# Order of the first batch's loads, room for four pooled weight tiles, and ScalarE alone for the upper halves of the weights

## The chip, the cores and the metric

One core of one Trainium2 chip runs the whole program. The metric is the device time of one execution in microseconds (us), as the median of several runs. TensorE (PE) multiplies, ScalarE (ACT) and VectorE (DVE) do most of the element-wise work, GpSimd (POOL) takes a share of it, and SyncE (SP) issues nearly all transfers (DMA) from one in-order queue. Each engine runs its own instructions in the order in which the program lists them, and waits on semaphores for the others.

## The reference

Three blocks follow each other: an attention over `[4, 8, 576, 64]`, then two feed-forward blocks over its 2304 x 512 output.

```python
def _attn_ref(q, k, v):
    ...
    q_d = q.reshape(B, H, Sd, factor, D).mean(axis=3)      # factor = 4, the same for k and v
    out_d = sm_attn(q_d, k_d, v_d)
    out_up = np.repeat(out_d, factor, axis=2)
    ...
    mask = np.abs(pos[:, None] - pos[None, :]) < factor
    scores = scale * np.matmul(q, k.transpose(0, 1, 3, 2))
    scores = np.where(mask, scores, -1000000000.0)
    ...
    return (out_up + out_local).astype(np.float32)

def _moe_ref(x, w_in, w_out):
    h = x @ w_in                                           # 512 -> 2048
    g = np.where(h > 0.0, h, alpha * (np.exp(np.minimum(h, 0.0)) - 1.0))
    return (g @ w_out).astype(np.float32)

def _moe2_ref(x, w_gate, w_val, w_out):
    g = x @ w_gate                                         # 512 -> 1536
    silu = g * (1.0 / (1.0 + np.exp(-g)))
    val = x @ w_val
    return (silu * val @ w_out).astype(np.float32)
```

The five weight matrices arrive as float64; everything else is float32.

## The kernel before

**Attention.** A batch is cut into six units of 96 positions (`add_unit`). A unit loads queries and keys (L459), TensorE turns them (L495), a copy puts them into `qT`/`kT`, groups of four positions are summed into `sums` (L506 on VectorE, L508/L509 on GpSimd), banded scores follow (L523), a softmax over 32 columns (L535 to L558), a copy of the turned weights into a block-diagonal tile `bd`, and the product with the values (L577), copied to `xf` (tile `f`). The pooled attention has four head pairs per batch (`add_pooled`): values of four neighbours summed into `vs` (L596, L600/L601), scores (L617), maxima (L624), exponentials (L630), weights divided by their sums (L640, tile `pr`), turned (L655), times `vs` (L668), kept in `xdT`. `add_split` then adds the two (L688) into `x`, three units to a chunk of 288 positions.

**First feed-forward block.** There are eight chunks c, each with 16 steps f of 128 hidden columns. Chunk 0 (`add_whole`) is multiplied in full float32 (L735 into `h`, L740 into the accumulator), while the float64 weights are still arriving: two words per number are joined by ScalarE (L374, L377) and VectorE (L381, L383) into one float32 tile per matrix and step, 32 tiles in all ("a pair" below is one L381 and one L383). Chunks 1 to 7 use three fast products per matrix (L710 to L712) on weights split into an upper part (a rounded copy, `copy` at L276 on ScalarE or L278 on VectorE) and a remainder (L421 on GpSimd); `add_weight_split` makes both. `x` of these chunks is split in the same way (copy, L698), and so is `g` (copy, L790).

**Order.** Nothing is issued in the order of the loops. Each piece of work is a task with an engine (or a choice of two), an estimated cost and a due time. `Work.run` plays the tasks out once while the program is built: an engine that comes free takes the ready task with the smallest due time whose buffers have room, and that fixes each engine's instruction order. Due times of the first block count from `START` in steps (`time1`). `spans` gives, for batches 1 to 3, the steps between which their attention is due; `add_unit` holds their turns back until a named weight tile is joined (`then`). Once the first product of chunk 0 is placed, all attention work shares two PSUM banks, 4 and 5 (`att_bank`), which the joining of the weights uses too.

**Room.** 33 slots of 4 KB per partition (`w0` to `w32`) serve in turn as landing place for the first batch (`parts`, from slot `U0` on), for float64 words (14 slots), for joined tiles, and for split weights. The first batch's queries, keys, values and pooled values all have places of their own there, so its loads wait for no earlier work.

Of the kernel before, what the change touches and what calls it, by code (L numbers as in the profile page):

```python
# [228 lines left out]
def attention_moe_moe(ctx: ExitStack, tc: tile.TileContext, q, k, v, w_in, w_out, w_gate, w_val, w_o2, ident_in, mask_in, band_in, picks_in, out):  # L229
# [19 lines left out]
    NW = 2 * NF1 + 1  # L249
    U0, U1 = 6, 19  # L250

# [53 lines left out]

    START, STEP0, STEP, STEP2 = 62.0, 4.1, 3.7, 7.9
    order = [(c, f) for c in range(NC) for f in range(NF1)]
# [106 lines left out]

    def add_weight_split(key, due, w):

        wt[key] = w
        u = ww[key]
        add(COPIER, (0.6, 0.4), due - 2, lambda engine: copy(engine, w.t[:, 0], u.t.bitcast(F32)),
            reads=[u], writes=[w], second=0)  # L420
        return add("pool", 1.3, due - 1, lambda: nc.gpsimd.tensor_tensor(  # L421
            out=w.t[:, 1], in0=u.t.bitcast(F32), in1=w.t[:, 0], op=ALU.subtract), reads=[u, w], writes=[w])
# [15 lines left out]
            ("mx", [HALF, 2, 2], 4), ("nm", [HALF, 2, 2], 4), ("su", [HALF, 2, 2], 4),  # L438
            ("pr", [HALF, 2, 2, G], 2), ("prT", [HALF, 2, 2, G], 2),
            ("sm", [P, H, QB], 2), ("st", [P, H, 1], 2), ("pt", [P, H, QB], 1))}  # L440
# [23 lines left out]

    def add_unit(n, due, load_due, rows=None, after=(), then=(), late=0.0):

# [18 lines left out]

        add("sp", 2.0, load_due + 4.0, load_values, writes=[tv], nbytes=P * H * D * 4 * 1.9, after=after)
        if i == 0:
# [97 lines left out]

    def add_pooled(b, p, due, load_due, raws=None):

        if xdT[b] is None:
            xdT[b] = xdT_ring.new()
        vs = vs_ring.new()  # L590
        mx, nm, su, pr, prT = (small[n].new() for n in ("mx", "nm", "su", "pr", "prT"))
        qk = sums[b]
# [53 lines left out]
        add("dve", 0.6, due + 4, norm, reads=[su], writes=[su])  # L646
        add(EITHER, (0.78, 1.75), due + 4.3, weight, reads=[pr, su], writes=[pr])

# [31 lines left out]
    def add_split(n, xf, due):  # L680
        b, i = divmod(n, NU)
        c, j = divmod(n, UPC)
        if j == 0:
            xt[c] = x_ring.new()
        x, cols = xt[c], slice(j * U, (j + 1) * U)

        def both(engine, to):
            two(engine).tensor_tensor(  # L688
                out=to.rearrange("p a (g r) -> p a g r", r=R), in0=xf.t.rearrange("p (a g r) -> p a g r", a=NP, r=R),
                in1=xdT[b].t[:, :, i * GU:(i + 1) * GU].rearrange("p a (g o) -> p a g o", o=1).to_broadcast([P, NP, GU, R]),  # L690
                op=ALU.add)

        f = lambda: xf.t.rearrange("p (a t) -> p a t", a=NP)
        if c == 0:
            return add(EITHER, (0.8, 1.4), due, lambda engine: both(engine, x.t[:, :, 0, cols].bitcast(F32)), reads=[xf, xdT[b]], writes=[x])
        add(EITHER, (0.8, 1.4), due, lambda engine: both(engine, f()), reads=[xf, xdT[b]], writes=[xf])
        add(COPIER, (0.5, 0.6), due + 0.3, lambda engine: copy(engine, x.t[:, :, 0, cols], f()), reads=[xf], writes=[x], second=1)
        return add("pool", 1.1, due + 0.6, lambda: nc.gpsimd.tensor_tensor(  # L698
            out=x.t[:, :, 1, cols], in0=f(), in1=x.t[:, :, 0, cols], op=ALU.subtract), reads=[xf, x], writes=[x])
# [24 lines left out]
    def add_whole(f, due, acc, last):  # L724
# [18 lines left out]
        inner[:] = [add("pe", 4 * 0.51, due - STEP, gemm1, reads=[wi, x], writes=[h], after=inner)]  # L743
        add_weight_split(("in", f), time1(NF1 + f), w_slots.new(split_places))
        add("act", 0.45, due - URGENT, lambda: nc.scalar.activation(e.t, h.t[:, :T1], AF.Relu, scale=-1.0), reads=[h], writes=[e])
# [3 lines left out]
        last[0] = [add("pe", 4 * 0.51, due + STEP, gemm2, reads=[wo, g], writes=acc[0], after=last.get(0, ()), slack=1.0)]  # L749
        split_last = [add_weight_split(("out", f), time1(NF1 + f + 1), w_slots.new(split_places))]  # L750
        if f == NF1 - 1:
# [127 lines left out]
    with tc.manual_schedule():  # L879
# [10 lines left out]
        vals = [x for _ in range(NU // 2) for x in parts(2)]  # L890
        praws = [x for _ in range(NP) for x in parts(2)]
        for t in praws:
            t.t = t.t[:HALF].rearrange("p (h x) -> p h x", h=2)
# [21 lines left out]
        for n in range(NU):  # L915
            xfs[n] = add_unit(n, 4.0 * n, -40 + 2 * n, rows=(*rows[n], vals[n]), late=0.0 if n < UPC else 24.0)
            if n == 0:
                load_mask()
        for p in range(NP):
            add_pooled(0, p, 20.0 + 0.5 * p, -31 + p, raws=praws[2 * p:2 * p + 2])  # L920
        w1 = [(kind, f) for f in range(NF1) for kind in ("in", "out")]
# [10 lines left out]
        for n in range(UPC):  # L932
            made.append(add_split(n, xfs[n], 28.0 + 0.5 * n))
        spans = {1: (12, 24), 2: (41, 54), 3: (71, 84)}
        split = UPC
        for b in range(1, B):
            lo, hi = (time1(s) for s in spans[b])
            for i in range(NU):
                due = lo + (hi - lo) * i / NU
                xfs[b * NU + i] = add_unit(b * NU + i, due, due - 18, after=[words["in", 10 if b == 1 else NF1 - 1]],  # L940
                    then=[words["out", NF1 - 1]])
            for p in range(NP):
# [75 lines left out]
```

## Time and profile before

| what | us |
|---|---|
| median of 3 runs (1036.3 to 1039.7) | 1038.58 |
| the profiled execution, whole | 1041.44 |
| its span (first to last instruction in the trace) | 1039.6 |
| TensorE busy in the span | 998.2 |

The span is the part that the trace shows; the profiled execution took 1.8 us more than its span, and 2.9 us more than the median. TensorE is busy 96% of the span, and its granted clock averages 0.97 of full speed. A matmul at half clock counts as busy for twice as long, so what TensorE loses is seen in both: in idle time, and in stretches with a low clock.

### The profile page before, as it was taken

What the parts mean: (1) busy time and instruction counts of PE and PEld (TensorE: products, weight loads), DVE (VectorE), ACT (ScalarE), POOL (GpSimd) and SP (SyncE); (2) the same over time, 40 slices, a digit from 0 to 9 for tenths busy, and PEclk for the clock granted to TensorE, in tenths of its full rate; (3) what the DMA queues carried; (4) which work ended last, traced back from release to release, by engine and by line L of the source; (5) the groups of instructions that cost most, each with busy time, mean ns of one, the idle gap of its engine ahead of it and who ended that gap; (6) DMA issues with size and microseconds to landing.
All of it is one profiled execution on the core that took longest, in us unless ns stands there. A gap on an engine that the chain in (4) does not pass through costs nothing. (4 is left out here: it accounts for less than half of the span.)

```text
span 1039.6 us, 19385 instructions
## 1 busy us (share of the span) xinstructions
PE 998.2 (96%) x7540; PEld 870.3 (84%) x7540; DVE 526.0 (51%) x1080; ACT 404.1 (39%) x994; POOL 318.4 (31%) x375
## 2 busy tenths in 40 slices
PE   7679899989999999999999999999999999999998
PEld 5457689979999899899998888888888888888897
DVE  5978997786788777783124322232223222322232
ACT  4868455555555455555434521121112111211111
POOL 4432883572426343357258720010001000000000
PEclk8679999989999999999999999999999999999999
DMA  9995243464634564334024420020002000100000
GB/s 162 290 330 154 58 98 104 138 167 133 159 112 119 159 156 124 116 107 145 1 76 126 116 83 1 1 64 18 1 1 71 0 1 2 50 1 1 7 35 21
DMA packets 129004, 91.20 MB, mean 88 GB/s; under 512 B 73744, under 2 KB 116880, under 8 KB 128912
## 3 DMA queue, kind: packets, MB, share of 16 engines
q1 hardware_dynamic: 128768, 89.70, 31.6%
q8 instruction: 59, 0.97, 0.4%
q14 instruction: 33, 0.27, 0.1%
q10 hardware_dynamic: 144, 0.26, 0.1%
HBM read 71.06 MB, written 18.87 MB: 87 GB/s over the span
## 5 line engine op out<-in xcount | busy, mean ns | idle before, releaser
L710 PE MATMUL bank<-x,w 128*128 128x288 f32 (+2 forms) x928 | 318.1, 343 | 5.5 <-DVE e L783 5.4
L711 PE MATMUL bank<-x,w 128*128 128x288 f32 (+2 forms) x928 | 312.4, 337 | 0.4 <-POOL x L698 0.4
L712 PE MATMUL bank<-x,w 128*128 128x288 f32 (+2 forms) x928 | 311.6, 336 | 0.0
L856 DVE TENSOR_TENSOR e<-bank,e 128x512 f32<-128x512 f32 (+1 forms) x120 | 76.2, 637 | 260.7 <-ACT e L853 179.8
L710 PEld LDWEIGHTS bank<-x,w 128*128 128x128 f32 x928 | 175.8, 189 | 28.6 <-DVE e L783 8.5
L711 PEld LDWEIGHTS bank<-x,w 128*128 128x128 f32 x928 | 176.5, 190 | 17.2 <-POOL x L698 0.6
L712 PEld LDWEIGHTS bank<-x,w 128*128 128x128 f32 x928 | 176.3, 190 | 16.8
L790 POOL TENSOR_TENSOR g<-e,g 128x288 fp32r<-128x288 f32 x112 | 93.4, 834 | 175.2 <-ACT g L276 124.1
L710 PE MATMUL bank<-g,w 128*128 128x288 f32 x448 | 135.3, 302 | 0.0
L711 PE MATMUL bank<-g,w 128*128 128x288 f32 x448 | 132.8, 296 | 0.0
L712 PE MATMUL bank<-g,w 128*128 128x288 f32 x448 | 132.3, 295 | 0.0
L853 ACT ACTIVATE e<-bank 128x512 f32<-128x512 f32 (+1 forms) x60 | 33.2, 555 | 190.8 <-PE bank L712 190.8
L833 POOL TENSOR_TENSOR x<-x2r,x 128x512 fp32r<-128x512 f32 (+1 forms) x20 | 23.6, 1194 | 270.9 <-ACT x L832 270.9
L858 ACT CAST y<-e 128x512 fp32r<-128x512 f32 (+1 forms) x60 | 34.6, 577 | 154.3 <-DVE e L856 132.4
L710 PEld LDWEIGHTS bank<-g,w 128*128 128x128 f32 x448 | 84.8, 189 | 1.9 <-issue 1.2
L711 PE MATMUL bank<-w,y 128*128 128x512 f32 x216 | 85.7, 397 | 0.0
L711 PEld LDWEIGHTS bank<-g,w 128*128 128x128 f32 x448 | 85.3, 190 | 0.2
L710 PE MATMUL bank<-w,y 128*128 128x512 f32 x216 | 85.3, 395 | 0.0
L783 DVE SCALAR_TENSOR_TENSOR e<-e,bank 128x288 f32<-128x288 f32 x112 | 50.2, 449 | 69.4 <-ACT e L787 62.9
L712 PEld LDWEIGHTS bank<-g,w 128*128 128x128 f32 x448 | 85.0, 190 | 0.0
L712 PE MATMUL bank<-w,y 128*128 128x512 f32 x216 | 84.9, 393 | 0.0
L779 ACT ACTIVATE e<-bank 128x288 f32<-128x288 f32 x112 | 45.9, 410 | 100.1 <-PE bank L712 79.9
(115 smaller groups left out, 1410.3 us busy)
## 6 DMA issues: line engine op xcount, KB each, us to landing
wd<-mid SPq DMA_DIRECT2D x72, 128.0 KB
u<-wd SPq DMA_DIRECT2D x36, 256.0 KB
w<-in_moe_w_in_dram SPq DMA_DIRECT2D x16, 512.0 KB
w<-in_moe_w_out_dram SPq DMA_DIRECT2D x16, 512.0 KB
w<-in_moe_w_gate_dram SPq DMA_DIRECT2D x24, 256.0 KB
w<-in_moe_w_val_dram SPq DMA_DIRECT2D x24, 256.0 KB
w<-in_moe_w_out_dram SPq DMA_DIRECT2D x24, 256.0 KB
out_dram<-x2r SPq DMA_DIRECT2D x17, 256.0 KB
```

The costliest lines, as they stand in the source:

```text
L710: nc.tensor.matmul(ps, sh, mh, start=first, stop=False)
L711: nc.tensor.matmul(ps, sh, ml, start=False, stop=False)
L712: nc.tensor.matmul(ps, sl, mh, start=False, stop=last)
L779: nc.scalar.activation(e.t, h.t[:, :T1], AF.Relu, scale=-1.0)
L783: nc.vector.scalar_tensor_tensor(out=e.t, in0=e.t, scalar=-1.0, op0=ALU.add, in1=h.t[:, :T1], op1=ALU.max)
L790: add("pool", 0.82, due - URGENT, lambda e=e, g=g: nc.gpsimd.tensor_tensor(out=g.t[:, 1], in0=e.t, in1=g.t[:, 0], op=ALU.subtract), reads= ...
L833: add("pool", 1.3, due, lambda T=T, raw=raw, x=x: nc.gpsimd.tensor_tensor(out=x.t[:, 1, :T], in0=raw.t[:, :T], in1=x.t[:, 0, :T], op=ALU.s ...
L853: add("act", 0.6, due, lambda T=T, e=e, gate=gate: nc.scalar.activation(e.t[:, :T], gate.t[:, :T], AF.Sigmoid), reads=[gate], writes=[e], ...
L856: add("dve", 0.64, due, lambda T=T, e=e, x=x: nc.vector.tensor_tensor(out=e.t[:, :T], in0=x.t[:, :T], in1=e.t[:, :T], op=ALU.mult), reads= ...
L858: add("act", 0.6, due, lambda T=T, e=e, y=y: nc.scalar.copy(y.t[:, 0, :T], e.t[:, :T]), reads=[e], writes=[y])
```

## The change

The first batch's loads are asked for in another order: all queries and keys, then the rows for the pooled values, then the values of the units (`v_due`, and other due times in `add_pooled`). The four pooled weight tiles of the first batch get a place each in the slots (`probs`, so `U0` is 2 and `pr` has one buffer left for the later batches); their division by the sums, and the three additions into `x` of chunk 0, are VectorE's alone where VectorE or GpSimd could take them. The upper copies of the first block's weights are ScalarE's alone. `START` is 48 where it was 62, batch 1's attention is due in steps 10 to 20 where it was 12 to 24, and the turns of batches 1 to 3 are held back until the output tile of step 10 is joined, where it was that of step 15.

```diff
-    U0, U1 = 6, 19
+    U0, U1 = 2, 19
...
-    START, STEP0, STEP, STEP2 = 62.0, 4.1, 3.7, 7.9
+    START, STEP0, STEP, STEP2 = 48.0, 4.1, 3.7, 7.9
...
-    def add_weight_split(key, due, w):
+    def add_weight_split(key, due, w, copiers=COPIER):
...
-        add(COPIER, (0.6, 0.4), due - 2, lambda engine: copy(engine, w.t[:, 0], u.t.bitcast(F32)),
+        add(copiers, (0.62, 0.9)[:len(copiers)], due - 2, lambda engine="act": copy(engine, w.t[:, 0], u.t.bitcast(F32)),
...
-            ("pr", [HALF, 2, 2, G], 2), ("prT", [HALF, 2, 2, G], 2),
+            ("pr", [HALF, 2, 2, G], 1), ("prT", [HALF, 2, 2, G], 2),
...
-        add("sp", 2.0, load_due + 4.0, load_values, writes=[tv], nbytes=P * H * D * 4 * 1.9, after=after)
+        add("sp", 2.0, load_due + 4.0 if v_due is None else v_due, load_values, writes=[tv], nbytes=P * H * D * 4 * 1.9, after=after)
...
-        add(EITHER, (0.78, 1.75), due + 4.3, weight, reads=[pr, su], writes=[pr])
+        if b:
+            add(EITHER, (0.78, 1.75), due + 4.3, weight, reads=[pr, su], writes=[pr])
+        else:
+            add("dve", 0.78, due + 4.3, lambda: weight("dve"), reads=[pr, su], writes=[pr])
...
-            return add(EITHER, (0.8, 1.4), due, lambda engine: both(engine, x.t[:, :, 0, cols].bitcast(F32)), reads=[xf, xdT[b]], writes=[x])
+            return add("dve", 0.8, due, lambda: both("dve", x.t[:, :, 0, cols].bitcast(F32)), reads=[xf, xdT[b]], writes=[x])
...
-        add_weight_split(("in", f), time1(NF1 + f), w_slots.new(split_places))
+        add_weight_split(("in", f), time1(NF1 + f), w_slots.new(split_places), COPIER[:1])
...
+        probs = [x for _ in range(NP) for x in parts(1)]
...
-            xfs[n] = add_unit(n, 4.0 * n, -40 + 2 * n, rows=(*rows[n], vals[n]), late=0.0 if n < UPC else 24.0)
+            xfs[n] = add_unit(n, 4.0 * n, -40 + 2 * n, rows=(*rows[n], vals[n]), late=0.0 if n < UPC else 24.0,
+                v_due=-20.0 + n)
...
-            add_pooled(0, p, 20.0 + 0.5 * p, -31 + p, raws=praws[2 * p:2 * p + 2])
+            add_pooled(0, p, 16.0 + 0.5 * p, -28 + p, raws=praws[2 * p:2 * p + 2], pr=probs[p])
...
-        spans = {1: (12, 24), 2: (41, 54), 3: (71, 84)}
+        spans = {1: (10, 20), 2: (41, 54), 3: (71, 84)}
...
-                    then=[words["out", NF1 - 1]])
+                    then=[words["out", 10]])
```

(The same edit is made to the `out` weights.) What the planner makes of these numbers is seen in three places. First SyncE's queue, from its fourth load of the first batch on. `w_95` to `w_100` hold queries and keys of units 0 to 5, `w_101` to `w_103` values, `w_104` to `w_107` the rows for the pooled values. Before:

```order
L459 DMA w_96<-in_k_dram 112x8x64
L459 DMA w_101<-in_v_dram 16x8x64
L459 DMA w_101<-in_v_dram 13x8x64
L459 DMA w_101<-in_v_dram 32x8x64 x3
L459 DMA w_97<-in_q_dram 96x8x64
L459 DMA w_97<-in_k_dram 112x8x64
L459 DMA w_101<-in_v_dram 32x8x64 x4
L459 DMA w_98<-in_q_dram 96x8x64
L459 DMA w_98<-in_k_dram 112x8x64
L459 DMA w_102<-in_v_dram 32x8x64 x4
```

Now:

```order
L459 DMA w_97<-in_q_dram 96x8x64
L459 DMA w_97<-in_k_dram 112x8x64
L459 DMA w_98<-in_q_dram 96x8x64
L459 DMA w_98<-in_k_dram 112x8x64
L459 DMA w_99<-in_q_dram 96x8x64
L459 DMA w_99<-in_k_dram 112x8x64
L459 DMA w_100<-in_q_dram 96x8x64
L459 DMA w_100<-in_k_dram 112x8x64
L606 DMA w_104<-in_v_dram 72x2x256 x2
L606 DMA w_105<-in_v_dram 72x2x256 x2
L606 DMA w_106<-in_v_dram 72x2x256 x2
L606 DMA w_107<-in_v_dram 72x2x256 x2
```

All loads of values have moved behind these; the first weights still come after the last values, in both.

Second, VectorE just ahead of the additions into `x` of chunk 0 (L688 before, L692 now), on which the first product of the feed-forward block waits. Before, the first two CASTs being upper copies of weights:

```order
L278 CAST w_889<-w_763 128x512
L278 CAST w_894<-w_763 128x512
L381 SCALAR_TENSOR_TENSOR bank_887<-bank_887,w_799 128x512
L383 SCALAR_TENSOR_TENSOR w_799<-w_572,bank_887 128x512
L381 SCALAR_TENSOR_TENSOR bank_892<-bank_892,w_881 128x512
L383 SCALAR_TENSOR_TENSOR w_881<-w_579,bank_892 128x512
L278 COPY prT_920<-bank_919 72x288
L381 SCALAR_TENSOR_TENSOR bank_926<-bank_926,w_881 128x512
L383 SCALAR_TENSOR_TENSOR w_881<-w_587,bank_926 128x512
L381 SCALAR_TENSOR_TENSOR bank_944<-bank_944,w_917 128x512
L383 SCALAR_TENSOR_TENSOR w_917<-w_591,bank_944 128x512
L688 TENSOR_TENSOR x_969<-f_512,xdT_802 128x4x96
```

Now:

```order
L597 TENSOR_REDUCE vs_847<-w_107 72x128
L278 COPY prT_841<-bank_849 72x288
L558 STREAM_TRANSPOSE pt_867<-sm_539 128x256
L535 TENSOR_TENSOR sm_715<-bank_713,mask_86 128x128
L535 TENSOR_TENSOR sm_715<-bank_714,mask_86 128x128
L381 SCALAR_TENSOR_TENSOR bank_785<-bank_785,w_760 128x512
L383 SCALAR_TENSOR_TENSOR w_760<-w_518,bank_785 128x512
L540 TENSOR_REDUCE st_884<-sm_715 128x8
L692 TENSOR_TENSOR x_890<-f_579,xdT_807 128x4x96
L692 TENSOR_TENSOR x_890<-f_603,xdT_807 128x4x96
L692 TENSOR_TENSOR x_890<-f_682,xdT_807 128x4x96
```

Seven pairs stood ahead of the additions before, one does now; and the third addition, which stood in GpSimd's queue behind the additions for batch 1's pooled values, has moved here.

Third, TensorE where chunk 1 ends and chunk 2 begins (products with `g` belong to chunk 1, those with `x` to chunk 2; the rest is attention of later units). Before:

```order
L712 MATMUL bank<-g,w 128x288
L523 MATMUL bank<-kT,qT 32x32 x32
L577 MATMUL bank<-bd,vrows 64x96 x8
L495 MATMUL bank<-ident,rows 128x96 x4
L495 MATMUL bank<-ident,rows 128x112 x4
L523 MATMUL bank<-kT,qT 32x32 x32
L710 MATMUL bank<-x,w 128x288
L711 MATMUL bank<-x,w 128x288
```

Now:

```order
L716 MATMUL bank<-g,w 128x288
L577 MATMUL bank<-bd,vrows 64x96 x8
L523 MATMUL bank<-kT,qT 32x32 x32
L714 MATMUL bank<-x,w 128x288
L715 MATMUL bank<-x,w 128x288
```

The product with the values has moved ahead of the scores, and the second unit's turns and scores behind the first products of chunk 2.

## Rows read from the trace of the kernel before

**Rows 1.** The page, part 1: busy time of each engine.

```profile
PE 998.2 (96%) x7540; PEld 870.3 (84%) x7540; DVE 526.0 (51%) x1080; ACT 404.1 (39%) x994; POOL 318.4 (31%) x375
```

**Rows 2.** Windows: length; busy us of PE, PEld, DVE, ACT, POOL; PE clock; DMA.

```profile
9.49:56.20 46.71, 32.75 (x620) 26.02 (x620) 41.07 (x108) 34.01 (x99) 21.93 (x35) 0.66 1.01 257
106.30:134.86 28.56, 25.08 (x321) 18.81 (x320) 26.77 (x47) 11.89 (x28) 24.00 (x23) 0.94 0.29 64
580.00:1040.00 460.00, 455.48 (x2136) 376.66 (x2136) 123.81 (x197) 88.62 (x160) 32.16 (x28) 1.00 0.08 24
```

**Rows 3.** Timeline of TensorE, first feed-forward block: start us, duration us, instruction, idle before.

```profile
61.33 8.29 PE L735 MATMUL bank<-x,w 128*128 128x288 f32 x24 [4.90 <-POOL x L688]
69.45 2.10 PE L740 MATMUL bank<-g,w 128*128 128x288 f32 x8
71.39 2.10 PE L735 MATMUL bank<-x,w 128*128 128x288 f32 x8
```

**Rows 4.** Timeline of VectorE and GpSimd: additions into x, and what stands ahead.

```profile
55.18 1.02 DVE L688 TENSOR_TENSOR x<-f,xdT 128x384 f32<-128x384 f32 x2
...
58.00 0.72 POOL L600 TENSOR_TENSOR praw<-praw 72x256 f32<-72x256 f32 x1 [4.94 <-DMA praw<-in_v_dram]
...
60.42 0.86 POOL L688 TENSOR_TENSOR x<-f,xdT 128x384 f32<-128x384 f32 x1
```

**Rows 5.** Timeline of SyncE's queue: the first weight.

```profile
33.56 0.40 SPq L332 DMA_DIRECT2D w<-in_moe_w_in_dram  x1
```

**Rows 6.** Windows of the trace: the first batch's loads (last column GB/s).

```profile
0.00:10.00 10.00, 6.36 (x21) 2.91 (x22) 1.21 (x2) 1.76 (x2) 3.66 (x14) 1.00 0.72 121
10.00:20.00 10.00, 8.31 (x230) 6.82 (x229) 6.88 (x23) 5.07 (x12) 3.70 (x8) 0.54 1.18 193
20.00:30.00 10.00, 6.55 (x218) 5.10 (x215) 8.36 (x23) 6.15 (x16) 7.61 (x16) 0.95 1.00 182
```

**Rows 7.** Groups of VectorE's instructions, 9 to 61.4 us (busy us, mean ns).

```profile
L383 DVE SCALAR_TENSOR_TENSOR w<-w,bank 128x512 int32<-128x512 int32 x10 | 6.9, 688 | 0.3
L381 DVE SCALAR_TENSOR_TENSOR bank<-bank,w 128x512 int32<-128x512 int32 x10 | 6.9, 686 | 0.0
...
L555 DVE TENSOR_TENSOR sm<-sm,st 128x256 f32<-128x256 f32 x6 | 2.6, 427 | 0.1
...
L640 DVE TENSOR_TENSOR pr<-pr,su 72x576 f32<-72x576 f32 x1 | 0.8, 755 | 0.0
```

**Rows 8.** Groups of VectorE's instructions, 85 to 160 us.

```profile
L278 DVE CAST w<-w 128x512 fp32r<-128x512 f32 x14 | 13.5, 986 | 1.2 <-POOL w L421 1.2
...
L555 DVE TENSOR_TENSOR sm<-sm,st 128x256 f32<-128x256 f32 x5 | 4.6, 925 | 0.0
L278 DVE COPY bd<-pt 32x192 f32<-32x192 f32 x8 | 4.5, 564 | 0.1
```

**Rows 9.** Tile w and line L421: min/median/max ns, first and last start.

```profile
L278 DVE CAST w<-w x16: 393/848/1498, 48.9 to 145.9; 128x512 fp32r<-128x512 f32 x16
...
L276 ACT CAST w<-w x16: 607/618/622, 99.1 to 150.0; 128x512 fp32r<-128x512 f32 x16
...
L421 POOL TENSOR_TENSOR w<-w x30: 1270/1288/1543, 95.2 to 152.0; 128x512 fp32r<-128x512 f32 x30
```

**Rows 10.** Waits, 106 to 135 us: us in total, times, longest.

```profile
PE bank L735 <- DVE g L747: 2.6, 2, 2.0
```

**Rows 11.** Timeline of TensorE, end of chunk 1.

```profile
208.71 0.76 PE L523 MATMUL bank<-kT,qT 64*32 64x32 f32 x64
212.33 1.55 PE L577 MATMUL bank<-bd,vrows 128*64 128x96 f32 x16 [2.87 <-DVE sm L535]
...
217.39 0.61 PE L710 MATMUL bank<-x,w 128*128 128x288 f32 x1
```

**Rows 12.** Windows after the end of chunk 1.

```profile
212.30:217.40 5.10, 4.22 (x89) 3.29 (x89) 4.45 (x8) 1.90 (x6) 2.85 (x4) 0.50 0.50 150
217.40:222.40 5.00, 5.00 (x27) 4.98 (x23) 4.43 (x12) 1.95 (x7) 3.22 (x5) 0.50 0.90 233
```

More of the change, by code (lines that the diff above doesn't have):

```diff
@@ L463, in attention_moe_moe, with add_unit @@
     sums = {}
-    def add_unit(n, due, load_due, rows=None, after=(), then=(), late=0.0):
+    def add_unit(n, due, load_due, rows=None, after=(), then=(), late=0.0, v_due=None):
         b, i = divmod(n, NU)
@@ L584, in add_unit, with add_pooled @@
         return xf
-    def add_pooled(b, p, due, load_due, raws=None):
+    def add_pooled(b, p, due, load_due, raws=None, pr=None):
         if xdT[b] is None:
@@ L590, in add_pooled @@
         vs = vs_ring.new()
-        mx, nm, su, pr, prT = (small[n].new() for n in ("mx", "nm", "su", "pr", "prT"))
+        mx, nm, su, prT = (small[n].new() for n in ("mx", "nm", "su", "prT"))
+        pr = pr or small["pr"].new()
         qk = sums[b]
@@ L749, in add_whole @@
         last[0] = [add("pe", 4 * 0.51, due + STEP, gemm2, reads=[wo, g], writes=acc[0], after=last.get(0, ()), slack=1.0)]
-        split_last = [add_weight_split(("out", f), time1(NF1 + f + 1), w_slots.new(split_places))]
+        split_last = [add_weight_split(("out", f), time1(NF1 + f + 1), w_slots.new(split_places), COPIER[:1])]
         if f == NF1 - 1:
@@ L891, in attention_moe_moe @@
         praws = [x for _ in range(NP) for x in parts(2)]
+        probs = [x for _ in range(NP) for x in parts(1)]
+        for t in probs:
+            t.t = t.whole.t.rearrange("p a b -> p (a b)")[:HALF, :4 * G].bitcast(F32).rearrange("p (j u k) -> p j u k", j=2, u=2)
         for t in praws:
```

## The prediction

> **What bounds the kernel now.** The page's busy times come first: TensorE works for 998.2 us of the span [rows 1], and no other engine comes near. So the windows are read next, stage by stage, for stretches where TensorE is not full. From 580 us on it is busy for 455.48 of 460 us at full clock [rows 2]: nothing can be absorbed there, and what is won or lost earlier arrives at the end whole. The losses lie early, in three places.
>
> The first is the start. TensorE's timeline shows the first product of the feed-forward block at 61.33 us, after 4.90 us of waiting for an addition into `x` [rows 3]. VectorE had made two of the three additions at 55.18 to 56.20 us; the third stood in GpSimd's queue behind the summing of batch 1's pooled rows, which waited for a transfer until 58.00, and it ran only at 60.42 [rows 4]. VectorE itself, from 9.49 to 56.20 us, was busy for 41.07 of 46.71 us [rows 2]: it paces the first batch. The second place is the end of chunk 0, 106.30 to 134.86 us, where TensorE lacks 28.56 - 25.08 = 3.5 us [rows 2]; 2.6 us of that it waited for `g` from VectorE [rows 10]. The third is the step from chunk 1 to chunk 2: the product with the values waited 2.87 us, chunk 2 began at 217.39 [rows 11], and the clock stood at 0.50, the 1.2 GHz level, from 212.30 to 222.40 [rows 12].
>
> **The start.** I sum VectorE's work up to the additions, from the two orders. Six pairs less (7 to 1): 6 x (0.688 + 0.686) = 8.2 us. Five weightings of the softmax less, which GpSimd takes: 5 x 0.427 = 2.1 us. Three divisions more (they were one of four on VectorE, now all): 3 x 0.755 = 2.3 us [rows 7]. Two copies into `bd` more, eight pieces of 0.564 us = 4.5 us [rows 8]; that row lies in a stretch with a busy GpSimd, so 4.5 is the dear end, and I keep it. One addition more: half of 1.02 = 0.5 us [rows 4]. Of small copies, turns and reductions net eight less, taken at the 0.4 us of the smallest tensor operation of rows 7: 3.2 us. Sum: -8.2 - 2.1 + 2.3 + 4.5 + 0.5 - 3.2 = -6.2 us, so that `x` is whole at 56.2 - 6.2 = 50.0 us if VectorE idles as long as before, 46.71 - 41.07 = 5.6 us [rows 2].
>
> Does it? The new order of loads brings queries and keys sooner and the units' values later, and TensorE's queue has the products of units 0 and 1 with their values ahead of the pooled scores. Ahead of unit 1's last values stand 2.56 MB of queries and keys, 1.18 MB of pooled rows and 0.52 MB of values, 4.26 MB. The windows moved 1.21 MB in the first 10 us, 1.93 in the next, then 0.18 per us [rows 6]: 4.26 MB are there at about 26 us. With the two products at 1.55 us and a pooled score of 1 us the maxima can start near 29 us, where VectorE would arrive at 25 to 26 us. That is some 3.5 us of idle time, inside the 5.6 us. Bounds: 2 us of idle puts `x` at 46.4, twice as much as before at 55.7.
>
> The bytes ahead of the first weight are the same, so it comes no later than now, when it is asked for at 33.56 us [rows 5]. What is late next is the joining: before, ten pairs were made ahead of the first product [rows 7], now one. From `x` on VectorE makes three pairs (4.1 us), small work of 1.4 us and the first `g` (0.4 us): 50.0 + 5.9 = 55.9 us, and the first output product follows, after two inner ones. Before, it came at 69.45 after three [rows 3]; an inner product takes 71.39 - 69.45 = 1.94 us, so the lead is 69.45 - 55.9 - 1.94 = 11.6 us. After that a step costs TensorE 3.9 us and VectorE two pairs and a `g`, 3.2 us: it keeps up. By the additions alone the lead would be 61.33 - 50.1 = 11.2. I take **-11.3 us**, bounds -5.6 and -14.9.
>
> **End of chunk 0.** 14 upper copies, 13.5 us, leave VectorE here, at 0.99 us each [rows 8]; their fastest took 0.39 and their slowest 1.50, while all of ScalarE's took 0.61 to 0.62 [rows 9]. ScalarE gets 16 x 0.618 = 9.9 us more; in this stretch it is busy for 11.89 of 28.56 us [rows 2], which hides it; without that cover the copies would delay the remainders on GpSimd, and chunk 1. The waits for `g` have VectorE's queue as cause: of 2.6 us I take **-2.0**. Against it: batch 1's turns now begin while weights are still being joined in the same banks 4 and 5. No row shows that mixture. The nearest wait for one of those banks is 2.87 us [rows 11]; the lower end is nothing. Two waits of half that mean a little less than 3; since only some ten of the 32 pairs are left by then, I take half of it, **+1.5**. GpSimd's remainders ran from 95.2 to 153.3 us [rows 9], some 55 us ahead of chunk 1's end; a start 11 us earlier does not use that up.
>
> The Trainium skill, in "SBUF — State Buffer", section "Who interferes with whom", says that a VectorE instruction with two inputs in SBUF, or a copy in a two-port mode, and a GpSimd instruction that reads SBUF shut each other out for a whole instruction. The spread of rows 9 agrees for the copies. By that rule moving divisions and additions to VectorE is a risk, taken up among the rivals.
>
> **Chunk 1 to chunk 2.** Idle from 209.47 to 212.33, 2.9 us [rows 11]; idle 5.10 - 4.22 = 0.9 us; and 4.22 + 5.00 us of work at half clock, of which half, 4.6 us, is loss [rows 12]: 8.4 us in all. The waiting product stood behind scores whose two banks VectorE had yet to read out; now it stands ahead of them, and the first products of chunk 2 follow the scores. Late next may be `x` of chunk 2, whose chain (pooled result, addition, copy, remainder) is unchanged. Bounds 0 and -8.4; I take the middle, **-4.0**.
>
> **Sum.** -11.3 - 2.0 + 1.5 - 4.0 = -15.8 us. The profiled execution, 1041.4 us, would become 1025.6; it stands 2.9 us above the median, so the median becomes **1023 us**. What cannot be told from no change here is about 0.3%, 3 us.
>
> **Rivals.** (a) Only the start is won: the third place stays, and the end of chunk 0 gives back what it gains. For it: the chain to chunk 2's `x` still ends just at the boundary. 1038.6 - 11.3 = 1027 us; 0.22.
> (b) The values are the new wait: they land as late as the last loads, VectorE idles 11 us, `x` comes at 55.7. For it: the transfers are the slowest early, 121 to 193 GB/s [rows 6]. Against it: 4.26 MB, not all. 1038.6 - 5.6 = 1033 us; 0.10.
> (c) The seven operations with two inputs that are VectorE's now (four divisions, three additions) are slowed by GpSimd as L555 is, 0.925 against 0.427 [rows 7, 8]: 7 x 0.5 = 3.5 us, 1026 to 1027 us; 0.12. This is the rule of the page named above.
> (d) Slower: banks 4 and 5. Six units of batch 1 take four steps each through them while weights are joined, and TensorE waits in order. The end of chunk 1 shows 3.7 us over five such steps, 0.75 each [rows 11, 12]; 24 x 0.75 = 18 us, and a fall of the clock as in rows 12 costs 4.6 more. With the start's 11.3 and the 2.0 won: 1038.6 - 13.3 + 22.6 = 1048 us. It decides from a mean wait of 0.55 us. Against it: most of these steps come after the last pair. 0.06.
> (e) No change: chunk 1 starts early and waits for its split weights until its old time. Against it: the 55 us above. 1038 us; 0.03.
> The forecast, with some of each bound, holds 0.47.
>
> **Range.** The forecast alone reaches from all bounds good (-14.9 - 3.5 - 8.4 = -26.8, 1012) to 1030. With (a), (b) and (c) 1013 to 1034 holds more than 8 in 10. Faster: 0.47 + 0.22 + 0.10 + 0.12 = 0.91, cut to 0.90; within 0.3%: 0.04; slower: 0.06.
>
> **What would show it.** The first inner product near 50 us, directly after three additions on VectorE; no wait for `g` from L747's successor; upper copies on ScalarE at 0.62 us; idle under 2 us at the end of chunk 1 and full clock after it. A first product after 55 us, or TensorE waits on turns and scores of batch 1 that sum to more than 5 us before chunk 1, would make the prediction wrong.

## The result, and the profile after

The changed kernel takes 1025.63 us (median of 6 runs, 1023.43 to 1028.85) against 1039.8 us of the kernel before beside it: a ratio of 0.986, 95% interval 0.9828 to 0.9892. It is faster by 14.2 us; the forecast was 15.8 us less than the 1038.58 known then, 1023 us. The two profiled executions, from which the rows of the two kernels come, stand 12.6 us apart: 1041.44 and 1028.85 us, the latter the slowest of its six.

The page, part 1, of the changed kernel, which answers to [rows 1]:

```profile
PE 993.2 (97%) x7540; PEld 869.5 (85%) x7540; DVE 508.3 (49%) x1050; ACT 421.2 (41%) x1027; POOL 317.6 (31%) x368
```

Windows of the changed kernel, as in [rows 2, 12]: the first batch up to the last addition into `x`, the last 28.56 us of chunk 0, the half-clock stretch at the start of chunk 2:

```profile
9.49:53.83 44.34, 30.06 (x602) 24.73 (x600) 33.68 (x94) 26.28 (x82) 18.03 (x31) 0.65 0.92 237
93.03:121.59 28.56, 28.27 (x255) 22.03 (x253) 22.83 (x44) 23.76 (x51) 18.12 (x17) 1.00 0.35 72
203.51:209.60 6.09, 6.09 (x85) 5.75 (x86) 4.63 (x13) 2.58 (x7) 5.68 (x6) 0.50 0.69 202
```

The timelines of the changed kernel at the places of [rows 3, 4, 11]: TensorE's first inner and first output product, VectorE's three additions with GpSimd's two beside them, TensorE's first product of chunk 1, and the step to chunk 2:

```profile
53.98 6.87 PE L739 MATMUL bank<-x,w 128*128 128x288 f32 x16 [1.17 <-ACT sm L547]
60.68 2.10 PE L744 MATMUL bank<-g,w 128*128 128x288 f32 x8
...
51.24 2.59 DVE L692 TENSOR_TENSOR x<-f,xdT 128x384 f32<-128x384 f32 x3 [0.22 <-ACT xdT L276]
51.28 1.25 POOL L692 TENSOR_TENSOR f<-f,xdT 128x384 f32<-128x384 f32 x1 [3.69 <-ACT xdT L276]
53.46 1.10 POOL L692 TENSOR_TENSOR f<-f,xdT 128x384 f32<-128x384 f32 x1
...
121.59 0.40 PE L714 MATMUL bank<-x,w 128*128 128x288 f32 x1 [0.30 <-DVE g L751]
...
200.76 0.76 PE L523 MATMUL bank<-kT,qT 64*32 64x32 f32 x64 [1.90 <-DVE f L278]
203.51 0.61 PE L715 MATMUL bank<-x,w 128*128 128x288 f32 x1 [1.67 <-POOL x L702]
```

What the reader is to see, against the rows of before:

- The first product stands at 53.98 instead of 61.33 us [rows 3]: 7.35 us earlier, not 11.3. The first output product leads by 69.45 - 60.68 - 1.94 = 6.8 us.
- At the end of chunk 0 TensorE lacks 28.56 - 28.27 = 0.3 us, where it lacked 3.5 [rows 2]: 3.2 us of idle time won. The one wait for `g` left there is 0.30 us. The granted clock rose from 0.94 to 1.00 in this window, which is worth 25.08 x 0.06 = 1.5 us more: 4.7 us in all.
- At the step to chunk 2 it idles 1.90 + 1.67 = 3.6 us and then works 6.09 us at half clock, 3.0 us of loss: 6.6 us, where [rows 11, 12] gave 8.4. That is 1.8 us won.

7.35 + 3.2 + 1.8 = 12.35 us, and the profiled executions differ by 12.6. So the three places hold the main part of the change. That the sum is so close is partly chance: it leaves out the 1.5 us of clock, and by its first product the changed kernel has less attention behind it (80 products L577, five units, where 96, six units, stood ahead before).

Places in single executions also scatter, and the experiments must be read with that in mind. Five profiled kernels have the changed kernel's order on all engines up to the first product (the changed kernel, and below the runs with shared copies, with other queues at the step, and with the timing moved either way). It stands at 53.98, 52.94, 55.33, 55.27 and 53.19 us in them; with the order of the kernel before at 61.33, and at 62.38 in the run with the new timing. So the lead is known as 6.0 to 9.4 us only. Timelines of the run with shared copies, with other queues, and of the kernel before with the new timing:

```profile
52.94 6.33 PE L739 MATMUL bank<-x,w 128*128 128x288 f32 x16 [1.17 <-ACT sm L547]
...
55.33 6.88 PE L739 MATMUL bank<-x,w 128*128 128x288 f32 x16 [1.17 <-ACT sm L547]
...
62.38 2.29 PE L735 MATMUL bank<-x,w 128*128 128x288 f32 x4 [4.75 <-POOL x L688]
```

Durations of instructions, and distances inside one execution, are steadier than such places. The upper copies are all on ScalarE, and as short as predicted; groups of the changed kernel from 85 to 160 us, which answer to [rows 8, 9]:

```profile
L421 POOL TENSOR_TENSOR w<-w 128x512 fp32r<-128x512 f32 x32 | 42.0, 1333 | 24.6 <-ACT w L276 24.5
L276 ACT CAST w<-w 128x512 fp32r<-128x512 f32 x32 | 18.5, 617 | 0.1
```

### The profile page after: what moved, and what is told of

Read it like the earlier page. It is cut to its first block, busy times and chain, and to the rows that moved or that the text cites. A ratio compares the mean times of both kernels' runs of the same rounds, so it can differ in the third digit from the quotient of the medians.

```text
span 1026.9 us, 19357 instructions
## 1 busy us (share of the span) xinstructions
PE 993.2 (97%) x7540; PEld 869.5 (85%) x7540; DVE 508.3 (49%) x1050; ACT 421.2 (41%) x1027; POOL 317.6 (31%) x368
## 4 chain that ended last, share of the span: by engine, by line
PE 90%; DVE 4%; POOL 2%; ACT 1%; issue 1%; DMA 1%; SPq 0%; ACTq 0%; POOLq 0%; DVEq 0%
PE bank L714 27%; PE bank L715 26%; PE bank L716 26%; PE bank L739 3%; PE bank L744 3%; PE bank L577 2%; PE bank L495 1%; PE bank L523 1%; PE bank L672 1%; PE bank L659 1%; PE bank L618 1%; DMA wd<-mid 1%; POOL f L692 0%; DVE mid L353 0%; ACT bd L276 0%
```

## Experiments

Line numbers in rows are those of the kernel that a run starts from. The edits are of two kinds. In some kernels the order of every engine is kept, and an instruction is only given to another engine or held until a named other one is issued (`FORCED` and `HELD` below); what they show belongs to that instruction. In the others a due time or a room changes, and all work after it is placed anew. There the total also holds what the new placement does to chunks 3 to 7, so the verdict rests on the stage. The changed `START` needed no run: with 62 in the changed kernel, every engine's order is the same.

### The start

**The third addition alone.** Kernel before, order kept.

```diff
-            return add(EITHER, (0.8, 1.4), due, lambda engine: both(engine, x.t...
+            return add(EITHER, (0.8, 1.4), due, lambda engine: both("dve", x.t...
```

> The kernel before with its order kept, except that the third addition into x, which stood in GpSimd's queue until 60.42 us, is made by VectorE directly behind the other two. If this late addition alone is half of what the start gives, the first product comes at about 57.0 instead of 61.3 us and the time falls by 4 us, to 0.996. If the weights or their joining hold chunk 0 anyway, the first product comes as early, but the lead is gone by the tenth step and the time falls by less than 1.5 us.

Measured: 1034.2 us, ratio 0.9937 (0.9915 to 0.996). Timelines of VectorE and of TensorE in this run:

```profile
56.33 1.49 DVE L688 TENSOR_TENSOR x<-f,xdT 128x384 f32<-128x384 f32 x3
...
57.87 4.49 PE L735 MATMUL bank<-x,w 128*128 128x288 f32 x14 [0.28 <-DVE x L688]
```

The first product is 3.5 us earlier, although VectorE's additions begin 1.15 us later in this execution than before (56.33 against 55.18 [rows 4]); counted from there it is 4.6 us earlier. The time is 5.9 us less (4.2 to 8.8 by the interval): this one addition is a large part of the start. The lead isn't lost in chunk 0, although the waits for `g` grow from 2.6 to 4.3 us there. And the three additions take 0.50 us each: GpSimd ran nothing between 54.2 and 59.45 us.

**GpSimd quiet beside the additions.** Changed kernel, order kept; `("add", 3)` and `("add", 4)` are GpSimd's two additions in the rows above.

```diff
+HELD = {("add", 3): ("x", 2), ("add", 4): ("x", 2)}
+FORCED = {("add", 3): "dve", ("add", 4): "dve"}
```

> The changed kernel with its order kept, except that two additions which GpSimd made at 51.28 and 53.46 us, beside VectorE's three additions into x, are made by VectorE behind these. If GpSimd slows VectorE's additions, the three take 0.50 us each as in the run that moved only the third addition, not 0.86, and the first product comes 1 us earlier. If their operands make them slow, they stay at 0.8 to 0.9 us. The time should not move by more than 1 us.

Measured: 1023.8 us, a single run. Timelines of VectorE and of GpSimd:

```profile
50.60 1.84 DVE L692 TENSOR_TENSOR x<-f,xdT 128x384 f32<-128x384 f32 x3 [0.21 <-ACT xdT L276]
...
50.47 0.62 POOL L543 TENSOR_TENSOR sm<-sm,st 128x256 f32<-128x256 f32 x1 [3.52 <-DVE st L540]
```

The same three additions take 1.84 instead of 2.59 us. GpSimd's one instruction left there covers the first of them, and only 0.34 us over 3 x 0.50 remain. The durations repeat: 2.59 or 2.60 us in five other executions with GpSimd's two additions beside them, 1.84 again in the last run below. So GpSimd slowed them; the mechanism of rival (c) is real, at 1.1 us where the rival had 3.5, since the four divisions, most of them beside an idle GpSimd, took 0.73 to 0.75 us in the changed kernel, no longer than before (0.755 [rows 7]). The first product stands at 52.80 us, 1.2 us earlier, but more than half of that is scatter: counted from the start of the additions it comes 2.20 instead of 2.74 us later, 0.5 us less where 1 was expected. The Trainium skill, "SBUF — State Buffer", section "Who interferes with whom", says that a VectorE instruction with two inputs in SBUF contends with a GpSimd instruction that reads SBUF; the two rows agree, with 0.61 and 0.86 us for one addition.

**The fourth pair's chain first.** Changed kernel, order kept but for two pieces.

```diff
+HELD = {("bd", 3): ("div", 0, 1), ("rest", "in", 0): ("exp", 0, 3)}
```

> The changed kernel with two pieces moved in the first batch: on VectorE the copies of one unit into its block-diagonal tile stand behind the maxima of the fourth head pair, on ScalarE the first weight's words stand behind the fourth pair's exponentials. If the chain over the fourth pair (maxima 38.20, exponentials 39.80 to 41.2, turning 40.67 us) sets the start, the exponentials begin near 38.0, x is whole at about 51.9 instead of 53.75, and the time is 1.8 us under the changed kernel (0.984 of the kernel before). If the values' landing or the two-buffer chain of turn, product and sum behind it sets it, x is whole at 53.2 or later and the time is within 0.6 us of the changed kernel.

Measured: 1025.4 us, 0.9859 (0.9836 to 0.9883), no change. Timelines of ScalarE and of TensorE, and the window from 40.94 us to the end of the last products:

```profile
37.68 0.38 ACT L631 ACTIVATE w<-bank,nm 72x144 f32<-72x144 f32 x1 [0.68 <-DVE su L637]
...
40.94 0.69 PE L659 MATMUL bank<-ident,w 72*72 72x72 f32 x4 [1.36 <-DVE prT L278]
...
47.44 2.24 PE L672 MATMUL bank<-prT,vs 72*64 72x144 f32 x16
...
40.94:49.68 8.74, 8.74 (x68) 6.94 (x68) 6.05 (x15) 5.10 (x14) 2.16 (x4) 0.50 1.06 380
```

The exponentials of the fourth pair are 2.1 us earlier (39.80 before the edit). The last products of the pairs start 0.56 us earlier (48.00 before), which is inside the scatter; counted from VectorE's first maxima they start 47.44 - 31.16 = 16.28 us later here and 48.00 - 31.78 = 16.22 us later in the changed kernel, so nothing is won. The start came 4 us later than forecast, and my reading that the first weight in ScalarE's queue cost them falls. From 40.94 us on TensorE works without a gap on the turns and products of the pairs, one behind the other, at half clock (0.50 granted there); VectorE idles 2.7 us beside it.

**The old order of loads.** Changed kernel, placed anew.

```diff
-                v_due=-20.0 + n)
+                )
-            add_pooled(0, p, 16.0 + 0.5 * p, -28 + p, ...)
+            add_pooled(0, p, 16.0 + 0.5 * p, -31 + p, ...)
```

> The changed kernel with the old due times of the first batch's loads (each unit's values right behind its queries and keys); all work is placed anew. If the order of the loads brings the earlier start, x is whole at 56 us or later and the time is 3 us or more above the changed kernel (0.989 or more). If the start comes from the third addition and from the work taken off VectorE, x is whole between 52.5 and 55.0 us and the time is within 2 us of the changed kernel, unless a wait for g or for weights appears elsewhere in chunk 0.

Measured: 1028.7 us, 0.9892 (0.9866 to 0.9918). The first batch's window:

```profile
9.49:53.20 43.71, 32.33 (x604) 26.30 (x602) 35.88 (x98) 28.19 (x86) 16.03 (x27) 0.63 0.98 256
```

The additions on VectorE's timeline:

```profile
50.66 2.54 DVE L692 TENSOR_TENSOR x<-f,xdT 128x384 f32<-128x384 f32 x3
```

`x` is whole at 53.2 us, as early as with the new order (53.83): VectorE has 2.2 us more to do and idles 2.8 us less (43.71 - 35.88 = 7.8 against 44.34 - 33.68 = 10.7). The order of the loads, which gave the change its name, does not bring the start in this placement. The total rises by 3 us all the same, and the start is not where: from 140 to 260 us alone TensorE idles 6.8 us, against 3.6 in the changed kernel.

**The old room.** Changed kernel, two buffers for the pooled weights in place of the four of `probs`, placed anew.

```diff
-    U0, U1 = 2, 19
+    U0, U1 = 6, 19
-            ("pr", [HALF, 2, 2, G], 1), ("prT", [HALF, 2, 2, G], 2),
+            ("pr", [HALF, 2, 2, G], 2), ("prT", [HALF, 2, 2, G], 2),
```

> The changed kernel with two buffers for the pooled weights and the first batch from the seventh slot on, as before; all work is placed anew. If the four buffers bring the earlier start, x is whole 2 us later or more and the time rises by 2 us or more (0.988 or more). If they only gather all four pairs' turns and products behind one another on TensorE at half clock (40.7 to 50.2 us, where VectorE idles 2.5 us), x is whole as early as in the changed kernel and the time is within 1.5 us of it.

Measured: 1028.4 us, 0.9886 (0.986 to 0.9911). VectorE's and TensorE's timelines:

```profile
58.16 2.85 DVE L692 TENSOR_TENSOR x<-f,xdT 128x384 f32<-128x384 f32 x3 [0.26 <-ACT xdT L276]
...
61.06 3.25 PE L739 MATMUL bank<-x,w 128*128 128x288 f32 x6 [1.33 <-DVE x L692]
```

Windows of this run, then the same two of the changed kernel:

```profile
260.00:400.00 140.00, 137.71 (x1549) 130.34 (x1548) 109.85 (x264) 79.94 (x226) 59.46 (x75) 1.00 0.56 148
400.00:580.00 180.00, 178.57 (x1409) 172.03 (x1408) 86.67 (x181) 91.24 (x231) 102.45 (x104) 1.00 0.34 101
```

```profile
260.00:400.00 140.00, 136.43 (x1588) 129.07 (x1587) 106.73 (x252) 79.39 (x224) 64.24 (x86) 0.99 0.52 141
400.00:580.00 180.00, 176.43 (x1305) 170.26 (x1304) 85.09 (x173) 91.31 (x228) 101.78 (x100) 0.98 0.35 104
```

The first product stands at 61.06 us, where it stood before the change, although VectorE makes all three additions. VectorE's maxima of the third and fourth pair start at 43.52 and 46.08 us, against 33.63 and 38.20 in the changed kernel, and four joined pairs of weights stand ahead of the additions. So with the new due times the earlier start needs the room for four pairs. It is not the only way to an earlier start: the kernel before, without the room, reached 57.87 us with the third addition alone. The total rises by 2.7 us only, since this placement happens to lose some 8 us less from 260 to 580 us: 3.7 us of idle time, against 7.1 and some 5 at a lower clock. So the size of the start can't be read from this total; its place can.

### The upper copies

**Kernel before, all of chunk 0's upper copies on ScalarE,** order kept.

```diff
-lambda engine: copy(engine, w.t[:, 0], ...
+lambda engine: copy("act" if key[0] in ("in", "out") else engine, w.t[:, 0], ...
```

> The kernel before, every instruction in its old place, except that the 16 upper copies that VectorE made in chunk 0 are made by ScalarE. If VectorE's upper copies cause the loss at the end of chunk 0 (the prediction's step), the 2.6 us of waits for g there go and the time falls by 2.0 to 3.5 us, to about 0.997 of the kernel before. If the changed kernel's gain in chunk 0 came from elsewhere (the attention of batch 1 that now stands later), the waits stay or turn into waits for ScalarE, and the time moves by less than 1 us (0.999 to 1.001).

Measured: 1035.3 us, 0.9956 (0.9939 to 0.9974). TensorE's waits for `g` from 61 to 147 us, and the last 28.56 us before its first product of chunk 1, which answer to [rows 2]:

```profile
PE bank L735 <- DVE g L747: 0.6, 1, 0.6
...
102.70:131.26 28.56, 26.48 (x334) 20.04 (x333) 19.83 (x41) 19.32 (x43) 25.09 (x25) 1.00 0.30 64
```

The waits for `g` fall from 2.6 to 0.6 us, and with the clock at 1.00 this window loses 28.56 - 26.48 = 2.1 us where it lost 3.5 + 1.5 = 5.0. From the first product (60.61 us) to the first of chunk 1 it takes 70.65 us, with the same work in between that took 73.53 before.

**Changed kernel, the 16 copies of the output weights back on VectorE,** order kept.

```diff
-lambda engine="act": copy(engine, w.t[:, 0], ...
+lambda engine="dve" if key[0] == "out" else "act": copy(engine, w.t[:, 0], ...
```

> The changed kernel with its order kept, except that the upper copies of the 16 output weights are made by VectorE again. If the copies decide, waits for g come back at the end of chunk 0 and the time is 2 to 3.5 us above the changed kernel, about 0.989 of the kernel before. If they don't, it stays within 1 us of the changed kernel (0.985 to 0.987).

Measured: 1032.9 us, 0.9937 (0.9914 to 0.9961), 7.3 us above the changed kernel. TensorE's timeline:

```profile
123.36 0.61 PE L714 MATMUL bank<-x,w 128*128 128x288 f32 x1 [3.10 <-DVE g L751]
123.77 0.44 PE L715 MATMUL bank<-x,w 128*128 128x288 f32 x1
124.01 0.44 PE L716 MATMUL bank<-x,w 128*128 128x288 f32 x1
```

The group of these copies from 85 to 160 us:

```profile
L278 DVE CAST w<-w 128x512 fp32r<-128x512 f32 x15 | 14.2, 949 | 0.0
```

Two windows:

```profile
100.00:120.00 20.00, 20.00 (x219) 15.64 (x218) 19.75 (x36) 11.54 (x25) 16.98 (x15) 1.00 0.22 47
120.00:140.00 20.00, 16.37 (x228) 13.85 (x226) 18.42 (x38) 9.88 (x26) 14.58 (x13) 0.83 0.33 74
```

Both runs point to the copies, the second well beyond the 2 to 3.5 us expected (the first, 4.8 us, is 2.7 to 6.3 by its interval). VectorE is full from 100 to 120 us (19.75 of 20), `g` comes late, and TensorE's wait of 3.10 us is followed by products 0.24 us apart, half clock (0.14 apart in the changed kernel at 121.83). From 120 to 140 us 3.6 us are idle and 16.37 x 0.17 = 2.8 are lost to the clock.

### The step from chunk 1 to chunk 2

**The timing of batch 1 alone, in both directions,** placed anew. In the kernel before and, reversed, in the changed one:

```diff
-        spans = {1: (12, 24), 2: (41, 54), 3: (71, 84)}
+        spans = {1: (10, 20), 2: (41, 54), 3: (71, 84)}
-                    then=[words["out", NF1 - 1]])
+                    then=[words["out", 10]])
```

> The kernel before with only the timing of batch 1's attention changed (due over steps 10 to 20, its turns held until the eleventh output weight is joined); all work is placed anew. If the old timing costs the same at the end of chunk 1 whatever the start is, the time falls by 4 us or more (0.996 or less) and the half-clock stretch at the step to chunk 2 gets shorter. If VectorE is the limit of chunk 0 in the kernel before, the attention that comes earlier only lengthens chunk 0 there, more than 3.5 us of idle time stand at its end, and the time is within 2 us of the kernel before or above it.

> The changed kernel with batch 1's attention timed as before (due over steps 12 to 24, its turns held until the last weight is joined); all work is placed anew, the first 50 us should not change. If the earlier turns in chunk 0 cost waits in banks 4 and 5 (the prediction's +1.5), chunk 0 ends no later than at 121.6 us and the time falls by 1 to 2 us. If they save the attention a crowded end of chunk 1, the idle time at the step to chunk 2 grows from 3.6 to 6 us or more and the time rises by 2 to 4 us (0.988 to 0.990).

Measured: the kernel before with the new timing 1032.1 us, 0.9924 (0.9902 to 0.9946); the changed kernel with the old timing 1035.1 us, 0.9948 (0.9929 to 0.9966). Windows from 140 to 260 us of the kernel before, of it with the new timing, of the changed kernel with the old timing, and of the changed kernel:

```profile
140.00:200.00 60.00, 59.35 (x610) 54.71 (x609) 46.14 (x117) 33.83 (x106) 30.70 (x34) 1.00 0.39 108
200.00:260.00 60.00, 56.28 (x609) 53.72 (x607) 45.32 (x94) 31.44 (x82) 32.23 (x44) 0.91 0.60 157
```

```profile
140.00:200.00 60.00, 60.00 (x664) 55.53 (x640) 48.41 (x105) 35.43 (x112) 32.78 (x39) 1.00 0.44 118
200.00:260.00 60.00, 58.44 (x654) 56.62 (x655) 44.31 (x102) 33.81 (x87) 25.60 (x34) 1.00 0.55 141
```

```profile
140.00:200.00 60.00, 57.70 (x592) 53.49 (x591) 44.97 (x103) 33.30 (x102) 31.64 (x33) 0.97 0.35 92
200.00:260.00 60.00, 53.66 (x581) 50.05 (x580) 43.97 (x96) 31.12 (x80) 30.05 (x42) 0.89 0.59 153
```

```profile
140.00:200.00 60.00, 58.86 (x618) 54.51 (x616) 45.80 (x99) 34.03 (x105) 34.61 (x38) 1.00 0.39 100
200.00:260.00 60.00, 57.57 (x676) 55.71 (x676) 44.79 (x106) 34.71 (x88) 26.26 (x35) 0.94 0.57 153
```

Count idle time, and busy time times what the clock lacks. The kernel before loses 0.65 + 3.72 + 56.28 x 0.09 = 9.4 us here, with the new timing 1.6: 7.8 less, and the time falls by 7.1. The changed kernel loses 7.0, with the old timing 16.3: 9.3 more, and the time rises by 9.4. Of all edits this one moves the time most. With the old timing the start (first product at 55.27 us, inside the scatter of the changed kernel) and the copies are still won, but this stage takes most of it back: it loses 16.3 us behind the early start, where it lost 9.4 behind the late one, and some 5 us are left by the ratio, where the changed kernel has 14. Of the run on the kernel before the first theory holds; of the other the second, well beyond the 2 to 4 us expected.

**Two steps earlier still.** Changed kernel, placed anew.

```diff
-        spans = {1: (10, 20), 2: (41, 54), 3: (71, 84)}
+        spans = {1: (8, 17), 2: (41, 54), 3: (71, 84)}
-                    then=[words["out", 10]])
+                    then=[words["out", 8]])
```

> The changed kernel with batch 1's attention two steps earlier still (due over steps 8 to 17, its turns held until the ninth output weight is joined); all work is placed anew. If the step from chunk 1 to chunk 2 still has 3.6 us of idle time because this attention is late, the time falls by 2 to 4 us (0.982 to 0.984 of the kernel before). If VectorE has no room left in chunk 0, waits for g or for banks 4 and 5 of 3 us or more come back at its end and the time is 2 us or more above the changed kernel.

Measured: 1029.6 us, 0.9894 (0.9871 to 0.9918), 4 us above the changed kernel. Waits of TensorE from 120 to 260 us (us in total, times, longest):

```profile
PE bank L714 <- DVE e L787: 2.9, 3, 1.7
PE bank L577 <- ACT kT L276: 1.8, 1, 1.8
```

The second theory holds in its size, but the waits are for `e` and `kT`, not for `g`.

**The queues at the step itself.** Changed kernel, order kept but for this place: one addition of chunk 2 on VectorE, three sums of batch 2 behind the remainders of `x` on GpSimd, one copy into `f` on ScalarE.

```diff
+HELD = {("sum", 12, 1): ("rem", 8), ("sum", 13, 0): ("rem", 8), ("sum", 13, 1): ("rem", 8)}
+FORCED = {("add", 6): "dve", ("f", 11): "act"}
```

> The changed kernel with its order kept except at the step from chunk 1 to chunk 2: one addition for chunk 2 moves from GpSimd to VectorE, three sums of batch 2's queries and keys stand behind the three remainders of x on GpSimd, and one unit's copy into f moves from VectorE to ScalarE. If these three queues cause the idle time there (1.90 us ahead of the scores, 1.67 us ahead of the second product), both waits fall under 0.7 us, the clock stays at full speed, and the time is 4 to 6 us under the changed kernel (0.980 to 0.982 of the kernel before). If something else is late next (the upper part of x on ScalarE, or the banks), the idle time only moves and the time is at most 1.5 us lower.

Measured: 1025.6 us, 0.9861 (0.9835 to 0.9888). Two windows of this run:

```profile
140.00:200.00 60.00, 60.00 (x628) 55.70 (x626) 46.81 (x103) 34.67 (x107) 31.49 (x35) 1.00 0.38 99
200.00:260.00 60.00, 56.54 (x717) 53.86 (x716) 47.13 (x107) 35.77 (x91) 27.72 (x39) 1.00 0.60 155
```

The waits of TensorE from 200 to 276 us (us in total, times, longest):

```profile
PE bank L714 <- DVE e L787: 2.1, 2, 1.2
PE bank L523 <- ACT f L276: 0.6, 1, 0.6
PE bank L495 <- DVE sm L535: 0.5, 1, 0.5
```

The two waits are gone and the clock stays full, but 60 - 56.54 = 3.46 us of idle time stand here, against 3.6 from 140 to 260 us before the edit, now as several small waits, two of them for VectorE's `e`. The windows give 7.0 - 3.5 = 3.5 us less loss; the median does not show it, and an effect of 2 us would not be resolved. That it only moves is the nearer theory.

### The three small moves together

The changed kernel, order kept, with the `HELD` and `FORCED` entries of the first chain, of the quiet GpSimd and of the step to chunk 2 together.

> The changed kernel with its order kept and three small moves together: the fourth head pair's chain first, GpSimd quiet beside the additions into x, and the queues at the step from chunk 1 to chunk 2. One by one they moved the first product by 0.6 and 1.2 us and chunks 1 and 2 by 1.9 us in the trace. If they add up, the time is 3 to 3.5 us under the changed kernel (0.9825 of the kernel before); if VectorE's queue gives each back later, it is within 1 us of it.

Measured: 1024.7 us, 0.9852 (0.9826 to 0.9878). The lowest median of several runs here, but 1 us under the changed kernel cannot be told from none: the second theory holds. The 0.6 and 1.2 us that the expectation adds up were places in single executions; by the distances above they are nothing and 0.5 us. No version clearly beats the changed kernel.

## Why the prediction was right, and which steps were not

The time fell into the range, 2.6 us above the forecast. That it is so near is partly luck: by the rows two terms were too large, by 3.95 and 2.2 us, and one too small by 2.7. (The 1030 us that the range calls the forecast's upper end is no sum of its bounds either: a start of -5.6 alone gives 1033.)

**The start, -11.3, was over-sized: 7.35 us at the first product,** 6.0 to 9.4 with the scatter. The work that leaves VectorE was counted right in sum: 41.07 - 6.2 = 34.9 us were expected and 33.68 measured. The step that failed is the idle time, "some 3.5 us of idle time, inside the 5.6": it is 44.34 - 33.68 = 10.7 us. TensorE's first product with the values and VectorE's first maxima in the changed kernel, and two windows: up to the maxima, and TensorE's turns and products of the pairs:

```profile
26.58 1.55 PE L577 MATMUL bank<-bd,w 128*64 128x96 f32 x16 [1.46 <-POOL half L508]
31.78 0.82 DVE L625 TENSOR_REDUCE mx<-bank 72x2 f32<-72x288 f32 x2 [1.68 <-PE bank L618]
...
9.49:31.78 22.29, 14.93 (x405) 12.81 (x405) 14.84 (x46) 10.06 (x24) 11.45 (x22) 0.65 0.91 165
40.67:50.24 9.57, 9.43 (x72) 7.37 (x72) 6.90 (x17) 6.60 (x20) 2.17 (x4) 0.50 1.06 379
```

Most of the idle time, 22.29 - 14.84 = 7.5 us, stands ahead of the first maxima: they start at 31.78 us, not near 29, and these 2.8 us are most of the 3.8 by which `x` came late (53.83 against 50.0). (With this order the first maxima start at 30.66 to 31.78 us, depending on the execution.) From there to the whole `x` it took 53.83 - 31.78 = 22.05 us, where the prediction left 21. In this part TensorE, in order, makes the turns and products of the pairs, which now come in a bunch, at half clock and almost without a gap (9.43 of 9.57 us), and VectorE idles 2.7 us beside it; the slowed additions are 1.1 us. Idle time is where rival (b) put it (11 us), yet the values' late landing is not its cause alone: with the old order of loads `x` is whole as early. What holds TensorE ahead of the first maxima stays open: in this execution the trace names GpSimd for 1.46 us, in two others with the same order so far the landing of the values (0.45 to 1.04 us a wait). What brings the start is the third addition on VectorE and, with these due times, the room for four pairs; how much each weighs in the changed kernel was not separated further. The sign "a first product after 55 us" was too sharp: two of the five executions passed it.

**The end of chunk 0, -2.0 + 1.5, was under-sized: 3.2 us of idle time won, 4.7 with the clock.** No wait in banks 4 and 5 shows before chunk 1; the +1.5 did not come, and rival (d) neither. The step that failed is that the copies' term was counted from the waits for `g` alone: the waits stood in a window with the clock at 0.94, which cost 1.5 us more [rows 2]. Put in alone or taken out the copies are worth 4.8 and 7.3 us. That the second is larger because an earlier start leaves VectorE less time for the same work fits VectorE's 19.75 busy of 20 us there, but the intervals of the two overlap.

**Chunk 1 to chunk 2, -4.0: 1.8 us less between the two kernels, but the wrong question.** The product with the values waits no more, as the prediction had it, and `x` of chunk 2, which it named as possibly late next, is one of the two things that TensorE then waits for (1.67 us). The step that failed is "Bounds 0 and -8.4; I take the middle": it took 8.4 us as a fixed loss of which a part is cured. The timing edit cures 7.8 us in the kernel before, and in the changed kernel it prevents 9.3. What looks like a gain of 1.8 is the cure less what the rest of the change, the earlier start above all, adds at this place: 16.3 - 9.4 = 6.9 us with the old timing. Rival (a), that the third place stays, is true of the rows (6.6 of 8.4 us) and false of the edit. Alone the third addition, the copies and the timing are worth 5.9, 4.8 and 7.1 us, 17.8 in all, and the whole change 14.2. This suggests that the terms do not simply add up; with intervals of some 2 us each it does not show it.

## What to carry to other kernels

When a stage starts earlier, ask what the next in-order chain, here the next batch's attention on VectorE, will still end at: unless it is moved too, it takes the gain back at its own boundary, here 6.9 us. An engine that paces a stage is slowed by its idle time as much as by its work, so work taken off its queue counts only until another in-order queue becomes the chain. And where every edit lets a planner place all work anew, judge it by its stage and by runs that keep the order; the total of one run carries several us from elsewhere. Before a place in a trace is read to a microsecond, look at other executions with the same order: here the first product scattered by 2.4 us, while the three additions ahead of it took 2.59 or 2.60 us in each.

## What the runs showed of the hardware

A wait of 3.1 us on TensorE after a full-clock stretch cost nearly twice its length, as products at half clock followed (0.24 instead of 0.14 us apart); with the queues at chunk 2 sorted, about as much idle time in waits of at most 1.2 us left the clock at 1.00 from 200 to 260 us. The same three additions took 0.50, 0.61 and 0.86 us each as GpSimd was idle, busy during one of them, and busy beside them. Turns and small products that kept TensorE busy for 9.43 of 9.57 us ran at a granted clock of 0.50 throughout.
